# One table set for log and exp, copies of the first heads in two parts, and a second output bank, in an attention and FFN kernel

## The chip, the core and the metric

The kernel runs on one core of a Trainium2 chip. The metric is the device time of one launch in microseconds (us). The engines go by short names: PE is TensorE (PEld its weight loads), ACT is ScalarE, DVE is VectorE, POOL is GpSimd, SP is SyncE, which issues DMAs.

## The reference

Gated attention over 8 batches of 8 heads, 576 positions and 64 columns, and a SwiGLU block over its 4608 rows. In short:

```
scores = (q @ k.T) / sqrt(64)
cum    = cumsum(log(clip(f, 1e-4, 1)), axis=-1)
scores = where(causal, -1e9, scores + cum[:, None] - cum[None, :])
attn   = exp(scores - max); attn /= sum(attn) + 1e-9
x      = (attn @ v), heads side by side        # 4608 x 512
out    = (silu(x @ w_gate) * (x @ w_val)) @ w_out    # inner width 1536
```

Inputs and output are float32; the matmuls run in bfloat16.

## The kernel before

The program does not run loops on the chip. A planner in Python (`Plan`) takes some 1,600 operations with a list of what each waits for, an estimated cost on each engine that may run it, a key (its priority) and for some an earliest time (`ready`), and lays them out on the engines. What stands on an engine runs in that order; waits between engines are semaphores. The dictionary `ORDER` at the end overrides the keys of several hundred operations by number, so it fixes most of the order. Where the planner sees PE idle early on, it fills in warm-up matmuls (`dummy`, tile `idle`, L1272).

PSUM has eight banks, in the planner's pools: four `f` (`ps_119` to `ps_122`), two `s` for scores (`ps_123`, `ps_124`), one `o` for attention outputs (`ps_125`), one `t` for turned (transposed) tiles (`ps_126`).

The stages that matter here:

- Gates (`gates`): f is loaded, clipped on DVE, its log taken on ACT (L363), and summed by a scan on DVE (L367). DVE then makes rows (`hi`, `less`, `mid`, `low`, L372 to L383) that carry the sums as parts in bfloat16, so that matmuls can add them to the scores; `choose` (L392 on ACT, L394 on DVE) makes each head's rows for the second half. All of it is done in two parts, positions 0 to 255 and 256 to 575.
- Batch 0 takes a short way (`four`, `attention2`): POOL issues four loads (`ld_quad`, two head pairs each, tile `su`), k and q for g=0 and then for g=1; PE turns each in 64x64 pieces (`turn_two`, L563); ACT or DVE copies a turned bank of 576 columns straight into `QK` (`straighten_two`, L328 or L330). Scores of two heads at a time (`score2`, L722 to L734) need those copies and the gate rows. Block 0 of a head needs only positions 0 to 255 and the first part of the gates, and is done for all heads first (tiles `PTa`).
- After each score comes the exp on ACT (`expo`, L738), a causal mask on POOL (`mask`, L747), the product with V on PE (`weigh`, L761), then DVE takes the reciprocal (L768) and scales (L773), which frees the `o` bank. The result goes into `xT`, by PE (`flip`, L778) and a copy (`put`), or by DMA later on.
- Batches from 1 on: q and k are turned by PE (`quad`, batch 1) or by DMA; `attention` takes one head at a time, with four blocks of scores (L704).
- The FFN takes rows of `xT` in tiles of 512, 512 and 128: gate product (L919, `wg`), tanh on ACT (L930), value product (L919, `wv`), products on DVE, then the out product (L985 and others). Silu is made from tanh at first and by ACT's Silu later on. FFN work of earlier batches is laid between the attention of later ones, and fills PE.
- ACT works with one table set of functions at a time. Before, a warm-up activation with Ln (L523) and one with Exp (L531) make the compiler put the table loads there; tanh is in the second set.

The loads that the first 50 us need stand on POOL's queue between POOL's masks: q and k of batch 0, V of batch 0, `wv`, `wg` and `wo` in parts, q and k of batch 1, V of batch 1 (partly as casting loads, `ld_vb`, into tile `VB`).

Of the kernel before, what the change touches and what calls it, by code (L numbers as in the profile page):

```python
# [10 lines left out]
BF16 = mybir.dt.bfloat16  # L11
# [12 lines left out]
class Op:  # L24
    def __init__(self, eng, fn, after, behind, take, use, key, ready, dma):
        self.eng, self.fn, self.take, self.use = eng, fn, take, take + use
        self.key, self.ready, self.dma = key, ready, dma
        self.after = [a for a in after if a is not None]
        self.behind = list(behind)
        self.next, self.then, self.wait = [], [], 0  # L30
        self.start = self.done = None
        self.late = False


class Plan:
# [41 lines left out]
    def run(self, idle=None):  # L77
# [15 lines left out]
        left, t, seq = len(self.ops), 0.0, 0  # L93
# [15 lines left out]
        while left:  # L109
# [4 lines left out]
            while events and events[0][0] <= t + 1e-9:  # L114
                _, _, kind, o = heapq.heappop(events)
                if kind in ("queue", "dma"):
                    for r, share in shares():
                        r[0][0] -= (t - moved) * share
                        while r and r[0][0] < 1e-6:
# [3 lines left out]
                            n.done = t + 1.0  # L123
# [32 lines left out]
            for e in engines:  # L156
                while busy[e] <= t + 1e-9:
# [26 lines left out]
                    if o.dma is not None:  # L184
# [3 lines left out]
                        push(max(end + (0.53 if o.tag == "f" else 0.9), T_SW if e == "POOL" else 0.0), "queue", o)  # L188
# [33 lines left out]
def kernel(ctx, tc, q, k, v, f, w_gate, w_val, w_out, out):  # L222
# [82 lines left out]
    def op(eng, fn, *args, tag=None, packet=20.0, raw=0.0, **kw):  # L305
# [3 lines left out]
        o.tag, o.packet, o.raw = tag, packet, raw  # L309
        return o  # L310
# [109 lines left out]
    def gates(parts, key):  # L420
# [5 lines left out]
        for i, c in enumerate(parts):  # L426
            w = c.stop - c.start
            a = op(("DVE", 0.03 + w / 960), clip, lf[:D], c, after=lds, key=key - 1 + 0.1 * i, tag="clip")
            a = op(("ACT", 0.13 + w / 1100), ln, lf[D:], c, lf[:D], after=[a], key=key + 0.1 * i, tag="ln")
            lns.append(op(("ACT", 0.13 + w / 1100), ln, lf[:D], c, after=[a], key=key + 0.1 * i + 0.01, tag="ln"))  # L430
# [92 lines left out]
    o_ln = op(("ACT", 1.5), lambda e: nc.scalar.activation(warm, warm, AF.Ln), key=-30,  # L523
# [7 lines left out]
    o_warm = op(("ACT", 1.4), lambda e: nc.scalar.activation(warm, warm, AF.Exp), after=lns, key=WARM_KEY)  # L531
    o_rest = op(("DVE", 0.3), blank, "rest", key=QKZ_KEY + 0.1)
    o_vb = [op({"DVE": 0.4, "ACT": 0.6} if i == 1 else ("DVE", 0.4 if i else 0.12), blank, i, after=[o_ct] if i == 1 else [], key=(-29.5, VB1_KEY)[i] if i < FIRST else 40 + 2000 * i, ready=0 if i == 0 else 4.5 if i < FIRST else 15) for i in range(NVB)]
# [23 lines left out]

    def turn_two(e, jj, x, bt):
# [88 lines left out]
    def four(g, key):  # L647
# [3 lines left out]
        for j in range(2):  # L651
            jj = 2 * g + j
            q_ready[0, jj] = []
            for x in range(2):
                kk = key + STEP[j] + x
                bt = Buf("t", ("f", TURN_F))
                o2 = op(("PE", 0.22), turn_two, jj, x, bt, after=[o1[x], o_id], take=[bt], key=kk, tag=("turn", 0, jj, x))
                turns.append(o2)
                q_ready[0, jj].append(op({"ACT": act(S), "DVE": dve(S) - 0.02}, straighten_two, jj, x, bt, after=[o2, o_qkz],
                                         use=[bt, hq2[0][g]], key=kk, tag=("str", 0, jj, x)))  # L660

    def quad(b, g, key, ready=0.0):
        done = [[], []]
        for x in range(2):
            kk = key + x
            o1 = op(("POOL", SW), ld_quad, b, g, x, key=kk, dma=1.45, packet=107, ready=ready, tag=("quad", b, g, x))
            for n, (t0, nt) in enumerate(PH):
                bt = Buf("t", ("f", TURN_F))
                o2 = op(("PE", 1.48 * mm(*[P] * nt)), turn, b, g, x, n, bt, after=[o1, o_id], take=[bt], key=S1_KEY + kk, tag=("turn", b, g, x))
# [164 lines left out]
    def attention2(b, key, parts):  # L834

        bx = {}
        for n, (bks, qb, nq) in enumerate(parts):
            ahead = len(parts) > 1 and n == 0
            got = {}
            for jj in range(4):  # L840
# [4 lines left out]
                for m, i in enumerate(bks):  # L845
                    bs = [Buf("s", ("f", F_UNTIL)) for _ in range(2)]
                    segs = [x[2] for x in BANKS[i]]
                    cost = mm(*segs) * (3 if jj in (ONEHOT1 if i else ONEHOT) else 2) + 0.105
                    gate_rows = [o_past] + dec0[0][jj] + (dec0[1][jj] if i else [])
                    a = op(("PE", cost), score2, b, jj, i, bs, after=q_ready[b, jj] + gate_rows, take=bs,  # L850
# [30 lines left out]
    def attention(p, key):  # L881
# [3 lines left out]
        for j in range(2):  # L885
            h = 2 * p + j
            bo, ws, x1 = Buf("o"), [], None
# [169 lines left out]
    def unit(t, fc, t0, n, hs, lo, kk, after):  # L1057
# [16 lines left out]
        else:  # L1074
            b = op(("ACT", act(n)), tanh, n, bg, bt, after=[g], take=[bt], use=[bg], key=-5, tag=("tanh", t, fc))
# [227 lines left out]
def pool2(n):  # L1303
# [28 lines left out]
STEP = (0, 2)  # L1332
# [7 lines left out]
WARM_KEY = -19.5  # L1340
# [5 lines left out]
TURN_F = 48.0  # L1346
# [94 lines left out]
```

## Time and profile before

| what | value |
|---|---|
| three runs | 376.00, 376.13, 375.93 us; median 376.0 |
| profiled execution | 376.5 us, of it a span of 374.5 us |
| PE busy | 368.0 us (98%) |
| DVE, ACT, POOL busy | 256.9, 212.5, 169.5 us |
| weight loads (PEld) | 249.2 us |
| granted TensorE clock | 1.0 |

The span runs from the first instruction to the end of the last; the rest of the profiled execution lies around it. A row of the timeline gives start, length, engine, line, operation, output tile and input tile, and in brackets the idle time of the engine before it with what ended it. Where rows of one kind follow each other they are merged (x4). Consecutive activations overlap, so the cost of one in a row of them is the distance from start to start.

### The profile page before, as it was taken

The numbers are of one execution on the slowest core, as the hardware profiler recorded it, in microseconds if no ns is written. First come the engines' busy times: TensorE is split into PE (matmuls) and PEld (weight loads), VectorE is DVE, ScalarE is ACT, GpSimd is POOL, SyncE is SP. The second block draws the span as 40 slices with busy tenths as digits, with TensorE's granted clock in tenths as the row PEclk, the third lists the DMA queues.
The fourth block names the chain that finished last, engine by engine and source line by source line (L and its number), as shares of the span: only waits on it lengthen the run. The fifth ranks groups of instructions, "written<-read, shape, count | busy, mean of one in ns | idle before, by whom it ended". The sixth has DMA issues, their size and how long they took to land.

```text
span 374.5 us, 9689 instructions
## 1 busy us (share of the span) xinstructions
PE 368.0 (98%) x3715; PEld 249.2 (67%) x3715; DVE 256.9 (69%) x605; ACT 212.5 (57%) x436; POOL 169.5 (45%) x396
## 2 busy tenths in 40 slices
PE   7899999999999999999999999999999999999996
PEld 5667666455789646875578955587666964584586
DVE  7878987499937699548973769845888246617633
ACT  6999953256755647756566556676874233333321
POOL 8897554135565416684249533566440400040021
PEclk9999999999999999999999999999999999999999
DMA  8999998896959997999979999898530120011012
GB/s 144 190 200 194 206 217 143 169 215 121 174 106 234 212 161 111 170 221 181 200 152 200 126 234 196 155 150 212 105 38 19 58 84 2 1 58 56 0 57 86
DMA packets 125179, 52.04 MB, mean 139 GB/s; under 512 B 111838, under 2 KB 119582, under 8 KB 124366
## 3 DMA queue, kind: packets, MB, share of 16 engines
q1 hardware_dynamic: 108638, 36.15, 50.8%
q0 software_dynamic: 16288, 15.14, 27.1%
q8 instruction: 29, 0.48, 0.6%
q14 instruction: 16, 0.13, 0.1%
q10 hardware_dynamic: 208, 0.14, 0.1%
HBM read 38.56 MB, written 17.07 MB: 149 GB/s over the span
## 4 chain that ended last, share of the span: by engine, by line
PE 93%; ACT 3%; DVE 2%; issue 1%; POOL 0%; DVEq 0%; ACTq 0%
PE ps L919 43%; PE ps L985 17%; PE ps L704 10%; PE ps L761 8%; PE ps L926 6%; PE ps L998 3%; PE ps L992 3%; PE ps L722 1%; PE ps L579 1%; PE ps L778 1%; ACT PT L738 1%; ACT QK L328 1%; PE ps L730 0%; ACT xT L363 0%; ACT PTa L738 0%
## 5 line engine op out<-in xcount | busy, mean ns | idle before, releaser
L738 ACT ACTIVATE PT<-ps 128x384 bf16<-128x384 f32 (+2 forms) x192 | 90.8, 510 | 15.6 <-PE ps L704 10.7
L919 PE MATMUL ps<-xT,wv 128*128 128x512 bf16 (+1 forms) x400 | 99.3, 370 | 0.0
L919 PE MATMUL ps<-xT,wg 128*128 128x512 bf16 (+1 forms) x400 | 99.1, 370 | 0.0
L943 DVE SCALAR_TENSOR_TENSOR hh<-th,ps 128x512 bf16<-128x512 f32 (+1 forms) x100 | 65.9, 662 | 19.4 <-PE ps L919 15.9
L930 ACT ACTIVATE th<-ps 128x512 f32<-128x512 f32 (+1 forms) x82 | 47.2, 577 | 51.5 <-PE ps L919 44.8
L747 POOL TENSOR_SCALAR_AFFINE_SELECT PT<-PT 128x128 bf16<-128x128 bf16 (+1 forms) x192 | 54.6, 291 | 41.6 <-ACT PT L738 35.9
L940 DVE SCALAR_TENSOR_TENSOR th<-th,ps 128x512 f32<-128x512 f32 (+1 forms) x82 | 53.7, 655 | 14.7 <-ACT th L930 14.4
L704 PE MATMUL ps<-QK 68*128 68x256 bf16 x392 | 62.8, 261 | 0.1
L919 PEld LDWEIGHTS <-wg 128*128 128x128 bf16 x400 | 37.7, 97 | 34.2
L919 PEld LDWEIGHTS <-wv 128*128 128x128 bf16 x400 | 37.4, 97 | 34.5
L747 POOL TENSOR_SCALAR_AFFINE_SELECT PTa<-PTa 128x256 bf16<-128x256 bf16 x64 | 26.9, 423 | 63.9 <-ACT PTa L738 62.9
L976 DVE TENSOR_TENSOR su<-hh 128x512 bf16<-128x512 bf16 (+1 forms) x126 | 46.6, 404 | 1.0
L985 PEld LDWEIGHTS <-su 128*128 128x128 bf16 x420 | 40.4, 98 | 5.3
L761 PE MATMUL ps<-VB,PT 128*128 128x65 bf16 x768 | 41.4, 193 | 0.1
L704 PEld LDWEIGHTS <-QK 68*128 68x128 bf16 x392 | 31.8, 97 | 13.9 <-issue 0.3
L1018 POOL TENSOR_TENSOR ot<-ot 128x256 f32<-128x256 f32 x14 | 10.1, 724 | 63.8 <-ACT ot L1011 63.8
L761 PEld LDWEIGHTS <-PT 128*128 128x128 bf16 x768 | 34.1, 97 | 7.0 <-POOL PT L747 1.0
L738 ACT ACTIVATE PTa<-ps 128x384 bf16<-128x384 f32 x64 | 30.9, 488 | 12.6 <-PE ps L704 11.7
L933 ACT ACTIVATE th<-ps 128x512 f32<-128x512 f32 x30 | 17.9, 596 | 33.1 <-PE ps L919 27.7
L773 DVE TENSOR_TENSOR xn<-ps,rc 128x320 bf16<-128x320 f32 (+2 forms) x72 | 32.4, 453 | 2.1
L985 PE MATMUL ps<-wt,su 128*128 128x256 bf16 x252 | 32.9, 272 | 0.0
L1011 ACT ACTIVATE ot<-ps 128x512 f32<-128x512 f32 x28 | 16.7, 597 | 27.9 <-PE ps L985 26.5
(101 smaller groups left out, 407.0 us busy)
## 6 DMA issues: line engine op xcount, KB each, us to landing
out_dram<-ot SPq DMA_DIRECT2D x35, 256.0 KB
natv<-in_v_dram SPq DMA_DIRECT2D x25, 256.0 KB
qk_d<-in_q_dram POOLq DMA_DIRECT2D x24, 144.0 KB, 4.3
qk_d<-in_k_dram POOLq DMA_DIRECT2D x24, 144.0 KB, 4.8
wv<-in_moe_w_val_dram POOLq DMA_DIRECT2D x3, 512.0 KB, 10.7
wg<-in_moe_w_gate_dram POOLq DMA_DIRECT2D x3, 512.0 KB, 12.1
wo<-in_moe_w_out_dram POOLq DMA_DIRECT2D x4, 384.0 KB, 13.7
VB<-in_v_dram POOLq DMA_DIRECT2D x7, 128.0 KB, 9.1
```

Of the source, the lines that this page charges most:

```text
L704: nc.tensor.matmul(s[:, c : c + w], QK[:KR, hqk[p].i, 1, j * S + kt * P : j * S + (kt + 1) * P], QK[:KR, hqk[p].i, 0, j * S + q0 : j * S + ...
L738: nc.scalar.activation(place(h, i)[:, OFFS[i] : OFFS[i] + c], ps(bs)[:, :c], AF.Exp, scale=0.125)
L747: nc.gpsimd.affine_select(out=d, in_=d, pattern=pat, compare_op=ALU.is_ge, fill=0.0, base=0, channel_multiplier=-1,)
L761: nc.tensor.matmul(o[:, lo : lo + D + 1], pt[:, c : c + P], VB[hvb[b].i][:, kt, hb, : D + 1], start=first and n == 0, stop=last and n == l ...
L773: nc.vector.tensor_mul(XN[bx.i][:, qb : qb + nq, j], o, r)
L919: nc.tensor.matmul(ps(bf)[:, a:b], w[:, ko, fc * P : (fc + 1) * P], xT[:, ko, at : at + b - a], start=ko == 0 and a == 0, stop=ko == KD - ...
L926: nc.tensor.matmul(ps(bf)[:, c * P : (c + 1) * P], w[:, ko, (4 * fq + c) * P : (4 * fq + c + 1) * P], xT[:, ko, lo : lo + P], start=c + ko ...
L930: nc.scalar.activation(TH[bt.i][:, :n], ps(bf)[:, :n], AF.Tanh, scale=0.5)
L940: nc.vector.scalar_tensor_tensor(out=t, in0=t, scalar=1.0, in1=ps(bf)[:, :n], op0=ALU.add, op1=ALU.mult)
L943: nc.vector.scalar_tensor_tensor(out=HH[bh.i][:, r, lo : lo + n], in0=TH[bt.i][:, :n], scalar=by, in1=ps(bf)[:, :n], op0=ALU.mult, op1=ALU ...
L976: E[e].tensor_tensor(out=o, in0=x, in1=y, op=f)
L985: nc.tensor.matmul(ps(bf)[:, c * HALF : (c + 1) * HALF], left(g)[:, q * P : (q + 1) * P], right[:, g], start=opens and g == 0, stop=g == K ...
```

## The change

Seven things change.

1. The first table load is named: the set `natural_log_exp_and_others`, which has Ln and Exp, is loaded at the start in place of the Ln warm-up. The second named load, `exp_and_others`, is planned from 24 us on, after the logs, and is waited for by the first FFN tile's tanh instead of by batch 0's first exps. Both warm-up activations go.
2. Batch 0's straightening copies are made in two parts, 29 of 64 column groups (29 x 9 = 261 columns) and the other 35 (315). Block 0 waits for the first parts only.
3. The turns of batch 0 take any `f` bank until 48 us, or `t`, where they took `t` first.
4. From 112 us (planned) a head's output may take the `t` bank, if `o` is held.
5. The planner's costs change: some for the logs, clips and loads, 0.095 us for a change between kinds of matmul on PE, casting loads (POOL's queue) that land between 9 and 20 us counted 0.7 us later.
6. `ORDER` is replaced as a whole, so most operations up to the last tile stand in another order.
7. A way to turn two head pairs in one go (`turn_four`, `straighten_four`) is added; `JOINED = ()` leaves it unused.

As built, ACT has 11 copies of batch 0 (six of 261 columns, five of 315) where it had six of 576, DVE five (two and three) where it had two; ACT has two `choose` rows where it had one and one 320-column `put` less. PE has 43 warm-up matmuls where it had 46 and the same matmuls otherwise; the last 720 stand in the same order of kinds. ACT's second table load stands behind all 32 exps of batch 0 and ahead of the first tanh. On POOL, the five loads of batch 0's V stand ahead of the first `wv`, the second of the second pair of q and k is q, and the last k load of batch 1 stands further back.

```diff
@@ Plan.run
-                            n.done = t + 1.0
+                            n.done = t + 1.0 + (0.7 if n.ran == "POOL" and 9.0 < t < 20.0 else 0.0)
...
+                        dur += SWITCH * (o.shape != shape)
+                        shape = o.shape
...
-    o_ln = op(("ACT", 1.5), lambda e: nc.scalar.activation(warm, warm, AF.Ln), key=-30,
+    o_ln = op(("ACT", 1.35), lambda e: nc.scalar.preload_act_table_set("natural_log_exp_and_others"), key=-30,
...
-    o_warm = op(("ACT", 1.4), lambda e: nc.scalar.activation(warm, warm, AF.Exp), after=lns, key=WARM_KEY)
+    o_warm = op(("ACT", 1.35), lambda e: nc.scalar.preload_act_table_set("exp_and_others"), after=lns, key=WARM_KEY, ready=WARM_AT)
...
+    EARLY = -(-HALF // QT)
...
-    def straighten_two(e, jj, x, bt):
+    def straighten_two(e, jj, x, c0, c1, bt):
         g, j = divmod(jj, 2)
-        dst = QK[:, hq2[0][g].i, x, j * S : (j + 1) * S].rearrange("p (c t) -> p c t", t=QT)
-        copy(e, dst, ps(bt).bitcast(BF16)[:, :S].rearrange("p (t c) -> p c t", t=QT))
+        dst = QK[:, hq2[0][g].i, x, j * S : (j + 1) * S].rearrange("p (c t) -> p c t", t=QT)[:, c0:c1]
+        copy(e, dst, ps(bt).bitcast(BF16)[:, :S].rearrange("p (t c) -> p c t", t=QT)[:, c0:c1])
@@ four
-                bt = Buf("t", ("f", TURN_F))
+                bt = Buf(*T_BANKS)
...
+                for m, (c0, c1) in enumerate(((0, EARLY), (EARLY, QP))):
...
+                        q_ready.setdefault((0, 2 * g + j), ([], []))[m].append(c)
@@ soft
-        a = x = op(("ACT", act(cols)), expo, h, i, bs, after=[a] + ([x1] if i > 1 else []) + ([o_warm] if h < H and not i else []),
+        a = x = op(("ACT", act(cols)), expo, h, i, bs, after=[a] + ([x1] if i > 1 else []),
@@ attention2
-                    a = op(("PE", cost), score2, b, jj, i, bs, after=q_ready[b, jj] + gate_rows, take=bs,
+                    a = op(("PE", cost), score2, b, jj, i, bs, after=q_ready[b, jj][0] + (q_ready[b, jj][1] if i else []) + gate_rows, take=bs,
@@ attention
-            bo, ws, x1 = Buf("o"), [], None
+            bo, ws, x1 = Buf("o", ("t", T_FREE, 1e9)), [], None
@@ unit
-            b = op(("ACT", act(n)), tanh, n, bg, bt, after=[g], take=[bt], use=[bg], key=-5, tag=("tanh", t, fc))
+            b = op(("ACT", act(n)), tanh, n, bg, bt, after=[g] + ([o_warm] if t == 0 else []), take=[bt], use=[bg], key=-5, tag=("tanh", t, fc))
@@ constants
-STEP = (0, 2)
+TURN_F = 48.0
+JOINED = ()
+COPY_ON = ("DVE", "ACT")
+T_FREE = 112.0
+T_BANKS = (("f", TURN_F), "t")
+SWITCH = 0.095
-WARM_KEY = -19.5
+WARM_KEY = -5.5
+WARM_AT = 24.0
 ORDER = {
...
```

More of the change, by code (lines that the diff above doesn't have):

```diff
@@ L31, in __init__ @@
         self.start = self.done = None
-        self.late = False
+        self.late, self.shape = False, None
 class Plan:
@@ L92, in run @@
         rings, moved = {"SP": [], "ACT": [], "POOL": []}, 0.0
-        left, t, seq = len(self.ops), 0.0, 0
+        left, t, seq, shape = len(self.ops), 0.0, 0, None
         events = []
@@ L187, in run @@
                         taken[k] += 1
-                        push(max(end + (0.53 if o.tag == "f" else 0.9), T_SW if e == "POOL" else 0.0), "queue", o)
+                        push(max(end + (0.73 if o.tag == "f" else 0.9), T_SW if e == "POOL" else 0.0), "queue", o)
                         push(busy[e], "wake", None)
@@ L309, in op @@
         o.tag, o.packet, o.raw = tag, packet, raw
+        o.shape = tag[0] if "PE" in eng and tag[0] in ("s2", "turn") else None
         return o
@@ L427, in gates @@
             w = c.stop - c.start
[L428 to L430 removed]
+            a = op(("DVE", 0.12 + w / 960), clip, lf[:D], c, after=lds, key=key - 1 + 0.1 * i, tag="clip")
+            a = op(("ACT", 0.18 + w / 980), ln, lf[D:], c, lf[:D], after=[a], key=key + 0.1 * i, tag="ln")
+            lns.append(op(("ACT", 0.18 + w / 980), ln, lf[:D], c, after=[a], key=key + 0.1 * i + 0.01, tag="ln"))
         for i, c in enumerate(parts):
@@ L650, in four @@
             o_id.behind.extend(o1)
[L651 to L655, printed above, removed]
-                bt = Buf("t", ("f", TURN_F))
-                o2 = op(("PE", 0.22), turn_two, jj, x, bt, after=[o1[x], o_id], take=[bt], key=kk, tag=("turn", 0, jj, x))
-                turns.append(o2)
-                q_ready[0, jj].append(op({"ACT": act(S), "DVE": dve(S) - 0.02}, straighten_two, jj, x, bt, after=[o2, o_qkz],
-                                         use=[bt, hq2[0][g]], key=kk, tag=("str", 0, jj, x)))
+        for x in range(2):
+            for n in range(2):
+                kk = key + x + 2 * n
+                bt = Buf(*T_BANKS)
+                if g in JOINED:
+                    o2 = op(("PE", 1.48 * mm(*[P] * PH[n][1]) - 0.09), turn_four, g, x, n, bt, after=[o1[x], o_id], take=[bt], key=kk, tag=("turn", 0, g, x, n))
+                else:
+                    o2 = op(("PE", 0.25), turn_two, 2 * g + n, x, bt, after=[o1[x], o_id], take=[bt], key=kk, tag=("turn", 0, g, x, n))
+                turns.append(o2)
+                for m, (c0, c1) in enumerate(((0, EARLY), (EARLY, QP))):
+                    w = (c1 - c0) * (2 * PH[n][1] if g in JOINED else QT)
+                    fn, args = (straighten_four, (g, x, n, c0, c1, bt)) if g in JOINED else (straighten_two, (2 * g + n, x, c0, c1, bt))
+                    on = {"ACT": act(w), "DVE": dve(w) - 0.02}
+                    c = op({COPY_ON[x]: on[COPY_ON[x]]} if g in JOINED else on, fn, *args, after=[o2, o_qkz],
+                           use=[bt, hq2[0][g]], key=kk + 50 * m, tag=("str", 0, g, x, n, m))
+                    for j in range(2) if g in JOINED else [n]:
+                        q_ready.setdefault((0, 2 * g + j), ([], []))[m].append(c)
     def quad(b, g, key, ready=0.0):
@@ L668, in quad @@
                 bt = Buf("t", ("f", TURN_F))
-                o2 = op(("PE", 1.48 * mm(*[P] * nt)), turn, b, g, x, n, bt, after=[o1, o_id], take=[bt], key=S1_KEY + kk, tag=("turn", b, g, x))
+                o2 = op(("PE", 1.48 * mm(*[P] * nt) - 0.09), turn, b, g, x, n, bt, after=[o1, o_id], take=[bt], key=S1_KEY + kk, tag=("turn", b, g, x))
                 turns.append(o2)
@@ L1345 @@
 V_CAST = {0: 5, 1: 3}
-TURN_F = 48.0
 DEC1_KEY = 1000
```

15 lines of the change are left out of this document (13 added, 2 removed), and 117 rows, old and new, of the table ORDER.

## Prediction

> **What bounds the kernel now.** I read the page first, then busy time by stage, then the timeline of the first 30 us, then the places where TensorE (PE) stands still later on. The page:
>
> ```profile
> span 374.5 us, 9689 instructions
> ...
> PE 368.0 (98%) x3715; PEld 249.2 (67%) x3715; DVE 256.9 (69%) x605; ACT 212.5 (57%) x436; POOL 169.5 (45%) x396
> ...
> PE 93%; ACT 3%; DVE 2%; issue 1%; POOL 0%; DVEq 0%; ACTq 0%
> ```
>
> PE has 368.0 of the 374.5 us and carries 93% of the chain that ended last. No edit takes a real matmul away: of the instructions on PE only three warm-up ones (L1272) go, 46 to 43. So only time in which PE stands still, warms up or waits can be won. The stages (window, PE, then weight loads, DVE, ACT, POOL):
>
> ```profile
> 0.00:16.00 16.00, 13.23 (x243) 9.90 (x245) 12.70 (x49) 12.38 (x26) 13.86 (x25) 1.00 1.24 162
> 16.00:36.00 20.00, 19.63 (x338) 13.96 (x333) 16.64 (x66) 19.68 (x45) 16.71 (x43) 1.00 1.42 196
> 36.00:112.00 76.00, 76.00 (x684) 48.00 (x683) 58.93 (x125) 43.74 (x95) 37.53 (x92) 1.00 0.92 169
> 112.00:288.00 176.00, 175.58 (x1793) 119.91 (x1791) 126.96 (x278) 110.81 (x231) 89.42 (x226) 1.00 0.94 164
> ```
>
> From 36 us PE is full: 76.00 of 76.00, then 175.58 of 176.00. Until then ScalarE (ACT) is the fullest engine: 19.68 of 20.00 us between 16 and 36. So the path runs over ACT to about 36 us and over PE from there; what ACT gains ahead of 36 us moves everything behind it. The last 720 matmuls stand in the same order in both kernels, so the end gives nothing. ACT's timeline and what feeds it (start, length, engine, line, operation; in brackets the idle time before it):
>
> ```profile
> 7.48 2.38 ACT L328 ACTIVATE QK<-ps 128x576 bf16<-128x576 bf16 x4
> ...
> 7.69 0.10 PEld L563 LDWEIGHTS <-su 64*64 64x64 bf16 x1 [0.78 <-DMA su<-in_q_dram]
> 8.05 0.40 DVE L360 TENSOR_SCALAR ot<-ot 128x216 f32<-128x216 f32 x1
> 8.16 0.66 PE L563 MATMUL ps<-ident,su 64*64 64x64 bf16 x36 [0.96 <-ACT QK L328]
> ...
> 8.38 0.86 DVE L367 TENSOR_TENSOR_SCAN xT<-xT 128x320 f32<-128x320 f32 x1
> ...
> 9.28 0.81 DVE L372 TENSOR_SCALAR xT<-xT 128x320 bf16<-128x320 f32 x1
> ...
> 9.40 0.34 PE L722 MATMUL ps<-QK 64*128 64x256 bf16 x4
> ...
> 9.74 0.38 ACT L363 ACTIVATE ot<-ot 128x216 f32<-128x216 f32 x1
> ...
> 10.14 1.28 ACT L531 ACT_TABLE_LOAD   x1
> ...
> 11.44 0.20 ACT L531 ACTIVATE warm<-warm 1x1 f32<-1x1 f32 x1
> 11.54 0.75 DVE L330 COPY QK<-ps 128x576 bf16<-128x576 bf16 x1
> 11.55 0.46 ACT L738 ACTIVATE PTa<-ps 128x384 bf16<-128x384 f32 x1
> 11.92 0.62 ACT L328 ACTIVATE QK<-ps 128x576 bf16<-128x576 bf16 x1
> ...
> 12.20 0.64 DVE L383 SCALAR_TENSOR_TENSOR xT<-xT,ct 128x320 bf16<-128x320 f32 x1
> 12.45 0.46 ACT L738 ACTIVATE PTa<-ps 128x384 bf16<-128x384 f32 x1
> ...
> 13.35 0.64 ACT L392 ACTIVATE xT<-xT,ct 128x320 bf16<-128x320 f32 x1
> ...
> 13.89 0.83 ACT L738 ACTIVATE PTa<-ps 128x384 bf16<-128x384 f32 x2
> ...
> 15.01 0.21 PE L733 MATMUL ps<-one,xT 64*128 64x128 bf16 x1 [0.68 <-issue]
> ...
> 15.31 1.82 ACT L738 ACTIVATE PTa<-ps 128x384 bf16<-128x384 f32 x4 [0.58 <-PE ps L734]
> ...
> 17.02 9.46 ACT L738 ACTIVATE PT<-ps 128x512 bf16<-128x512 f32 x22
> ...
> 26.54 0.44 ACT L328 ACTIVATE xT<-ps 128x320 bf16<-128x320 bf16 x1
> ...
> 29.00 0.37 ACT L930 ACTIVATE th<-ps 128x256 f32<-128x256 f32 x1
> ```
>
> The first scores begin at 9.40, but ACT loads the second table from 10.14 and the first exp runs at 11.55. Between 14.72 and 15.31 ACT idles 0.58 us: PE stood 0.68 us inside the second pair of scores (15.01), as I read it for a bank that the exps from 13.89 on were emptying. From 15.31 ACT runs on with hardly a gap; the first tanh is at 29.00.
>
> **Part by part.** All of it is costed on the profiled execution: 376.5 us, a span of 374.5 and 2.0 around it. The three runs have a median of 376.0, so I take the difference from there.
>
> *Table sets.* Both kernels load three tables. The second load moves from ahead of the first exp to behind the 32nd and last exp of batch 0, ahead of the first tanh. That takes 1.28 us away before 11.55 and puts 1.28 us back near 27 us, where ACT is as full. The warm-up activation goes: 11.44 to 11.55, 0.11 us won on ACT. Queued behind the moved load are the first tanh and the straightening copies of batch 1; PE waits for the tanh only once the banks of the gate products run out.
> The load's length is the row's: 1.28 us, and the idle time ahead of it is 10.14 less 9.74 and 0.38, that is 0.02 us. The Trainium skill, ScalarE: Activation LUTs, section What ACT_TABLE_LOAD costs, counts 1.28 us for the load and 1.38 us more for a drain at every change of set; the trace agrees with the first and shows nothing of the second. By the page's sum the moved load would save 2.66 us ahead of the first exp and cost 2.66 behind the last.
>
> *Copies in two parts.* Six ACT copies of 576 columns become six of 261 and five of 315; two of 576 on DVE become two of 261 and three of 315. ACT goes from start to start in 0.53 us with 576 columns (11.92 to 12.45) and 0.37 with 384 (11.55 to 11.92): 0.83 ns a column and 0.05 us fixed. So 6 x 0.27 + 5 x 0.315 = 3.2 us against 6 x 0.53 = 3.2: nothing, as DVE takes a part over. DVE went from start to start in 0.66 us with 576 columns (11.54 to 12.20). A part of 261 is between 0.30 (in proportion) and 0.66; I take 0.35, and 0.40 for 315, near the low end as ACT's fixed share is small too. DVE then does 1.9 us of copies for 1.3, ahead of 16 us, where it has 12.70 of 16.00. Block 0 needs only the first parts. Before, the turn of the first q waited until 8.16 for the bank that ACT had to empty, though the data were there at 7.69; now every turn has a bank of its own (four f banks, or t). The first scores then wait for DVE, which does the clip at 8.05, then two copies of 261 at 0.35 each: 9.1 instead of 9.40.
>
> *Exps.* Without the load, ACT ends its log at about 9.8 and starts the first exp there, 1.7 us earlier. The second q and k cannot land earlier (their loads stay third and fourth on POOL's queue), so the second scores gain less. In the new order ACT has ahead of the fifth exp four exps, four copies of 261, one of 315 and two gate rows (L392): 4 x 0.37 + 4 x 0.27 + 0.315 + 2 x 0.54 = 4.0 us from 9.8, so 13.8 against 15.31. The 0.58 us of idle time go, since these scores now take the s banks, which the first two exps have emptied. Four exps later (15.31 to 17.02 before, 1.7 us) the first exp of later blocks comes at 15.4 to 15.5 instead of 17.02, a lead of 1.6 us.
>
> *DVE's chain.* Those exps need the second half of the gate rows. On DVE the two copies of 261 now stand between the clip (8.05) and the scan (8.38), and two copies of 315 and two gate rows inside the chain, which ended at 12.84 (12.20 and 0.64); one copy of 576 leaves it. 2 x 0.35 + 2 x 0.40 - 0.66 for the copies, and for the gate rows 2 x 0.54 by ACT's row (the same columns): 12.84 + 1.9 = 14.8. It keeps up with 15.4 by 0.6 us, of which the scores take part.
>
> *ACT's sum to 36 us.* Load 0; warm-up -0.11; idle time -0.58; copies 0; one gate row more on ACT +0.54 (13.35 to 13.89); one 320-column put moved to DVE -0.44 (26.54). Sum -0.59 us. That the lead of 1.6 us comes down to 0.6 is the load paid later and the gate row. Bounds: -1.6 if PE finds enough other work during the load, +0.8 if the lead is lost (below).
>
> *Loads.* V of batch 0 now lies wholly ahead of the weights; wg stays behind wv and one q load of batch 1, with a k load moved behind it; the last k load of batch 1 moves on POOL's queue behind two V loads and sixteen masks, where it had two masks ahead of it.
>
> ```profile
> L919 PE MATMUL ps<-xT,wg x44: 269/272/380, 28.3 to 44.0; 128*128 128x256 bf16 x32, 128*128 128x512 bf16 x12
> L910 POOL DMA_DIRECT2D wg<-in_moe_w_gate_dram x3: 747/773/780, 12.4 to 31.6; - x3
> ...
> DMA to landing us min/median/max: 12.0/12.1/12.6
> ```
>
> wg is issued at 12.4, lands 12.0 us later at 24.4 and is first used at 28.3: 3.9 us of cover, and one 288 KB load fewer stands ahead of it. Cost nothing; without that cover PE waits as long as it is late. The last k load is needed only behind the first eight gate products of four matmuls, so after wg; by the same 12 us it lands near 32 if issued near 20. Cost nothing, +1 us at worst. The casting loads of V of batch 1 are issued later, behind most weights; the blocks that need them stand last in their head's products.
>
> *Second output bank.* From 112 us heads use the turns' bank for their outputs too. Before, each head opens the only o bank behind DVE's scaling of the head before. Where that was late:
>
> ```profile
> 129.48 0.49 DVE L773 TENSOR_TENSOR xn<-ps,rc 128x320 bf16<-128x320 f32 x1
> ...
> 130.03 0.12 PEld L761 LDWEIGHTS <-PTa 128*128 128x128 bf16 x2 [0.41 <-issue]
> ...
> 146.00 0.12 PEld L761 LDWEIGHTS <-PTa 128*128 128x128 bf16 x2 [0.19 <-issue]
> ...
> 150.45 0.12 PEld L761 LDWEIGHTS <-PTa 128*128 128x128 bf16 x2 [0.17 <-issue]
> ...
> 188.50 0.12 PEld L761 LDWEIGHTS <-PTa 128*128 128x128 bf16 x2 [0.20 <-issue]
> ...
> 274.07 0.21 PEld L761 LDWEIGHTS <-PT 128*128 128x128 bf16 x5 [0.27 <-POOL PT L747]
> ```
>
> The scaling ends at 129.97, the matmul goes on at once. The four gaps make 0.41 + 0.19 + 0.17 + 0.20 = 0.97 us, of which a weight load's 0.1 each would stand anyway: 0.6 us to win. The wait for a mask at 274.07 (0.27) is not of this kind and stays, and the new order sets some products a little closer behind their scores. I take -0.4, between -0.6 and +0.6 (two more mask waits of 0.3).
>
> Sum: -0.59 - 0.4 = -1.0 us: 375.5 in the profiled execution's terms, **375.0 us** against the median.
>
> **The rivals.**
> *The lead stays* (0.20): PE, not ACT, paces the stretch from 26 us, as the 19.63 of 20.00 us of PE also allow; the load hides behind products that are due anyway. Then -1.6 - 0.5 = -2.1: 373.9. Against it: ACT's 19.68.
> *Nothing is left* (0.17): ACT's idle time comes back at another bank (+0.58), and new mask waits eat the 0.4. Then 375.0 + 1.0 = 376.0.
> *Drain at the load* (0.05): an idle ACT ahead of the moved load while its pipeline empties, in the fullest stretch. Bounded by the row's 0.02 and, as a mechanism here, by the length of the load itself, 1.3: 375.0 + 1.3 = 376.3. By the Trainium skill's page above it would be 1.38 us.
> *Slower: DVE's chain is late* (0.20). The place is the copies ahead of the scan. If the low rows (L383, second half) end after about 16.5 instead of 14.8, the exps of later blocks begin no earlier than 17.0; the lead is gone while the load is still paid: +1.28 + 0.3 for the exps that shift - 0.44 - 0.11 = +1.0, and with -0.1 left of the bank 376.9. For it: the row at 9.28 took 0.81 us for 320 columns, more than the copy of 576 at 11.54, so DVE can be held up there; and DVE takes three more pieces.
>
> **How the numbers follow.** My forecast has 0.38; its own range, 374.6 to 375.5, is the ACT sum between -0.9 and -0.3 with the bank at its value. The range 373.7 to 376.9 reaches from the lead that stays to the late chain. A difference under 0.2% (0.75 us) is about what a measurement of this kernel can tell from no change. Faster by more, below 375.25: the lead and 0.30 of the forecast's 0.38, together 0.50. Within: the other 0.08 of the forecast, nothing left and the drain, 0.30. Slower, above 376.75: the late chain, 0.20.
>
> **What would show it.** First exp near 9.8 (11.0 would be a miss); first 512-column exp at 15.4 to 15.6; no idle ACT of 0.5 us between 13 and 17; table load at about 26 to 27 us with under 0.1 us of idle time ahead; first tanh within 1 us of before's 29.0; DVE's second low row ended by 15.0; no weight-load gaps behind DVE's scaling beyond 112 us. Wrong it is if the first 512-column exp comes after 16.5, if PE stands for a tanh behind the load for more than 1 us, or if mask waits past 112 us make more than 1.5 us.

## Result and the profile after

The changed kernel takes 374.36 us (median of 5 runs, 374.0 to 375.43) against 376.0 (375.9 to 376.43): a ratio of 0.9959, interval 0.9943 to 0.9975. Run again on another chip it gave 0.9969 (0.9958 to 0.9980). So it gains between 1.2 and 1.6 us; 1.0 was forecast. The profiled execution took 374.4 us, with a span 1.9 us shorter than before's. In some executions below, the clock granted to PE has a mean of 0.991 to 0.995 instead of 0.999 or 1.0 (full clock here), and before then has a median of 376.98 us (14 executions) against 376.23 (71), so differences at full clock stand beside the ratios.

The page, and busy time by stage (window, PE, weight loads, DVE, ACT, POOL):

```profile
span 372.6 us, 9646 instructions
...
PE 364.1 (98%) x3678; PEld 248.3 (67%) x3712; DVE 256.8 (69%) x608; ACT 212.7 (57%) x439; POOL 170.6 (46%) x396
...
16.00:36.00 20.00, 19.75 (x337) 15.15 (x334) 17.60 (x68) 19.84 (x44) 16.19 (x41) 1.00 1.33 200
...
112.00:288.00 176.00, 174.78 (x1771) 120.23 (x1789) 128.47 (x282) 109.97 (x230) 89.18 (x224) 1.00 0.92 161
```

ACT is still full between 16 and 36 us (19.84 of 20.00, 19.68 before). (Some matmul records are missing from this trace: 3678 beside 3712 weight loads. So its PE sums say nothing.) What changed is what ACT's full time holds. ACT's timeline:

```profile
8.73 0.76 ACT L331 ACTIVATE QK<-ps 128x315 bf16<-128x315 bf16 x2 [0.33 <-DVE QK L333]
...
9.65 0.87 ACT L762 ACTIVATE PTa<-ps 128x384 bf16<-128x384 f32 x2
...
11.78 0.39 ACT L331 ACTIVATE QK<-ps 128x261 bf16<-128x261 bf16 x1 [0.34 <-DVE QK L333]
...
14.10 0.53 ACT L762 ACTIVATE PTa<-ps 128x384 bf16<-128x384 f32 x1
14.84 1.25 ACT L762 ACTIVATE PTa<-ps 128x384 bf16<-128x384 f32 x3 [0.21 <-PE ps L758]
15.98 9.84 ACT L762 ACTIVATE PT<-ps 128x512 bf16<-128x512 f32 x24
25.84 1.28 ACT L534 ACT_TABLE_LOAD   x1
27.13 0.39 ACT L954 ACTIVATE th<-ps 128x256 f32<-128x256 f32 x1
27.41 1.53 ACT L331 ACTIVATE QK<-ps 64x640 bf16<-64x640 bf16 x2
```

The first exp comes at 9.65 instead of 11.55, the first 512-column exp at 15.98 instead of 17.02, and the first tanh at 27.13 instead of 29.00, though the whole table load of 1.28 us now stands ahead of it. ACT stands for 0.33, 0.34 and 0.21 us on the way. The load is entered without a pause: 24 exps end at 25.82, the load starts at 25.84.

PE and DVE ahead of 16 us, from the timeline of all engines:

```profile
8.75 0.34 PE L746 MATMUL ps<-QK 64*128 64x256 bf16 x4
...
10.66 1.08 DVE L333 COPY QK<-ps 128x315 bf16<-128x315 bf16 x2
...
13.94 0.55 DVE L386 SCALAR_TENSOR_TENSOR xT<-xT,ct 128x320 bf16<-128x320 f32 x1
...
14.24 0.23 PE L746 MATMUL ps<-QK 64*128 64x128 bf16 x2 [0.29 <-issue]
```

Scores start at 8.75 (9.40 before). DVE's second low row ends at 14.49. PE still stands inside the second pair of scores, for 0.29 us where it was 0.68.

Two profiles of one kernel differ too. In the second one of the changed kernel (span 373.5 us) the first tanh comes at 27.92. There the fourth q and k load landed at 11.19 us instead of 10.70. So 0.8 us of the difference between the two profiles first shown can be chance; where single profiles and times disagree, the times below decide.

### The profile page after: what moved, and what is told of

Its sections match the earlier page's. It is cut to its first block, busy times and chain, and to the rows that moved or that the text cites. A ratio compares the mean times of both kernels' runs of the same rounds, so it can differ in the third digit from the quotient of the medians.

```text
span 372.6 us, 9646 instructions
## 1 busy us (share of the span) xinstructions
PE 364.1 (98%) x3678; PEld 248.3 (67%) x3712; DVE 256.8 (69%) x608; ACT 212.7 (57%) x439; POOL 170.6 (46%) x396
## 4 chain that ended last, share of the span: by engine, by line
PE 71%; issue 0%; ACT 0%; POOL 0%; DVE 0%
PE ps L943 33%; PE ps L1009 17%; PE ps L728 8%; PE ps L950 6%; PE ps L785 5%; PE ps L1022 3%; POOL PTa L771 0%; ACT PTa L762 0%; ACT PT L762 0%; DVE ot L333 0%; PE ps L802 0%
## 5 line engine op out<-in xcount | busy, mean ns | idle before, releaser
L762 ACT ACTIVATE PT<-ps 128x512 bf16<-128x512 f32 (+2 forms) x192 | 90.4, 518 | 21.2 <-PE ps L728 16.4
L943 PE MATMUL ps<-xT,wv 128*128 128x512 bf16 (+1 forms) x386 | 97.8, 370 | 0.8
L943 PE MATMUL ps<-xT,wg 128*128 128x512 bf16 (+1 forms) x384 | 96.9, 370 | 0.8
L728 PE MATMUL ps<-QK 68*128 68x256 bf16 x392 | 64.0, 261 | 0.4 <-ACT PTa L762 0.2
L785 PE MATMUL ps<-VB,PT 128*128 128x65 bf16 x768 | 43.2, 193 | 0.1
L785 PEld LDWEIGHTS <-PT 128*128 128x128 bf16 x768 | 36.3, 97 | 9.3 <-POOL PT L771 1.0
L728 PEld LDWEIGHTS <-QK 68*128 68x128 bf16 x392 | 31.9, 97 | 12.8 <-issue 0.6
```

The source lines that it names most:

```text
L728: nc.tensor.matmul(s[:, c : c + w], QK[:KR, hqk[p].i, 1, j * S + kt * P : j * S + (kt + 1) * P], QK[:KR, hqk[p].i, 0, j * S + q0 : j * S + ...
L762: nc.scalar.activation(place(h, i)[:, OFFS[i] : OFFS[i] + c], ps(bs)[:, :c], AF.Exp, scale=0.125)
L785: nc.tensor.matmul(o[:, lo : lo + D + 1], pt[:, c : c + P], VB[hvb[b].i][:, kt, hb, : D + 1], start=first and n == 0, stop=last and n == l ...
L943: nc.tensor.matmul(ps(bf)[:, a:b], w[:, ko, fc * P : (fc + 1) * P], xT[:, ko, at : at + b - a], start=ko == 0 and a == 0, stop=ko == KD - ...
```

## Experiments

The theory of the prediction: ACT paces the kernel to 36 us, so the load costs the same wherever it stands, and the gain is idle time and a bank. The rival that the profile favours: the late load stands where ACT would have waited anyway. The twelve runs, with before and the first measurement, stand in one table; the ratio is to before on the same chip. The third column compares medians at full clock with before's on the same chip (4 to 12 executions of each variant). The start of the 17th tanh tells how the head went; the time from the 33rd to the 81st tanh holds most of the part in which the second output bank works. Single profiles scatter there: before and e7, whose work is in the same order, have 74.1 and 73.4 for the 17th tanh.

| kernel | ratio, interval | at full clock, us | 17th tanh, us | 33rd to 81st, us |
|---|---|---|---|---|
| before | 1 | 0 | 74.1 | 158.2 |
| after, first time | 0.9959 (0.9943 to 0.9975) | -1.6 | 72.4 | 157.7 |
| r_after: after again | 0.9969 (0.9958 to 0.9980) | -1.1 | 73.2 | 157.6 |
| e1: after, load early | 0.9982 (0.9971 to 0.9993) | -0.7 | 74.4 | 157.6 |
| e2: after, three loads | 1.0047 (1.0031 to 1.0062) | +1.1 | 75.4 | 158.3 |
| e3: after, one output bank | 0.9974 (0.9961 to 0.9988) | -1.1 | 72.2 | 158.1 |
| e4: after, whole copies | 0.9969 (0.9958 to 0.9980) | -0.8 | 73.3 | 157.8 |
| e8: after, load at tile 1 | 0.9962 (0.9951 to 0.9973) | -1.6 | 74.1, behind the load | 157.6 |
| e10: after, e1 + e3 + e4 | 0.9989 (0.9975 to 1.0003) | -0.7 | 73.2 | 158.4 |
| e11: after, a bank's copies on one engine | 1.0023 (1.0011 to 1.0036) | +0.8 | 74.5 | another order |
| e5: before, load late | 1.0028 (1.0017 to 1.0039) | +1.4 | 75.1 | 157.9 |
| e7: before, turns on the f banks | 0.9999 (0.9989 to 1.0009) | -0.2 | 73.4 | 158.2 |
| e9: before, e5 + e7 | 1.0013 (1.0005 to 1.0022) | +0.8 | 75.1 | 157.9 |
| e6: before, second output bank | 0.9974 (0.9962 to 0.9986) | -0.6 | 74.2 | 157.2 |

The changed kernel run once more was the yardstick of its variants:

> The changed kernel once more, as the mark for the others on the same chip: 0.994 to 0.998 of before in every theory.

### e1: the load back ahead of the first exp

```diff
@@ after: the planned operation emits nothing, the first exp emits the load
-    o_warm = op(("ACT", 1.35), lambda e: nc.scalar.preload_act_table_set("exp_and_others"), after=lns, ...)
+    o_warm = op(("ACT", 1.35), lambda e: None, after=lns, ...)
@@ expo
+        if not loaded:
+            loaded.append(nc.scalar.preload_act_table_set("exp_and_others"))
```

> The changed kernel (374.4 us) with one instruction moved: the load of the second table set stands ahead of the first exp again, and no longer ahead of the first tanh; every other instruction stands where it did on its engine. Theory A, the sum on record (ACT paces everything to about 36 us, so 1.28 us cost the same in both places): the first 512-column exp at about 17.3 instead of 16.0, the first tanh as before the edit, 374.1 to 374.7. Theory B (behind about 25 us PE is the pace and hides the late load): the first tanh stays near 27.1, but the exps and the products behind them run 1.0 to 1.3 later, 375.3 to 375.7.

Measured 0.9982: some 0.5 us slower than the changed kernel's second run, 0.9 than its first. The interval overlaps that of the second run; at full clock the medians are 375.49 and 375.15 us. ACT behind the last exps:

```profile
27.71 0.38 ACT L958 ACTIVATE th<-ps 128x256 f32<-128x256 f32 x1
29.38 1.55 ACT L331 ACTIVATE QK<-ps 64x640 bf16<-64x640 bf16 x2 [1.29 <-DVE rc L796]
```

and PE and DVE just before, in the timeline of all engines:

```profile
28.87 0.47 PE L596 MATMUL ps<-ident,xT 128*64 128x128 bf16 x10
...
29.19 0.17 DVE L796 RECIPROCAL rc<-ps 128x3 f32<-128x3 f32 x1
```

Where the late load stood, ACT now waits 1.29 us. The bracket names DVE's reciprocal, the last event before; what the copy reads is the turn of batch 1 that PE starts at 28.87 and ends at 29.34. So the load's room became a wait for PE. What stands ahead of 17 us in this profile can't be compared directly: the granted clock was 0.50 from 12.8 to 16.2 us, behind a wait of PE of 1.26 us, and 18 turns of PE that start at 12.90 took 0.69 us, not 0.47 as in the changed kernel. Half of e1's ten executions have a mean clock of 0.995, as this one; what brings the stretch on is not shown. The hole stands in e8 and e10 too, whose profiles are at full clock there. That the load costs less in the late place is what the times favour; how much less, they leave open between 0.3 and 0.9 us.

### e8: the load taken out of that place in another way

The first 16 tanh (tile 0's) are done as exps here, which need no new set, and the load stands ahead of the 17th; that tile's silu is thereby another function.

```diff
@@ tanh
+        made.append(n)
+        if len(made) == 17:
+            nc.scalar.preload_act_table_set("exp_and_others")
-        nc.scalar.activation(TH[bt.i][:, :n], ps(bf)[:, :n], AF.Tanh, scale=0.5)
+        nc.scalar.activation(TH[bt.i][:, :n], ps(bf)[:, :n], AF.Exp if len(made) < 17 else AF.Tanh, scale=0.5)
```

> The changed kernel with the second table load moved out of the head: the first FFN tile's 16 tanh are replaced by exp (so that tile's values are others), which the first set has, and the load stands ahead of the second tile's first tanh, near 72 us, where ACT has idle time; all else in its order. Theory A (ACT is the pace around 26 us): 1.0 to 1.3 us less than the changed kernel. Theory B (PE's products cover one load there, as the first tanh that came only 0.6 us later in the kernel with the early load suggests): within 0.3 us of the changed kernel, with ACT idle in the load's place.

Measured 0.9962, between the changed kernel's two ratios. Its profile and the second one of the changed kernel have the fourth load landing alike (11.10 and 11.19 us). First e8, then the changed kernel again:

```profile
26.51 0.38 ACT L959 ACTIVATE th<-ps 128x256 f32<-128x256 f32 x1
28.08 1.54 ACT L331 ACTIVATE QK<-ps 64x640 bf16<-64x640 bf16 x2 [1.19 <-DVE rc L792]
```

```profile
26.63 1.28 ACT L534 ACT_TABLE_LOAD   x1
27.92 0.38 ACT L954 ACTIVATE th<-ps 128x256 f32<-128x256 f32 x1
28.20 1.53 ACT L331 ACTIVATE QK<-ps 64x640 bf16<-64x640 bf16 x2
```

Without the load the tanh comes 1.41 us earlier, and then ACT waits 1.19 us; the copies of batch 1 start at 28.08 against 28.20. Of these 0.12 us none need be the load's: e8's tanh starts 0.12 us ahead of the other kernel's load already (26.51, 26.63), and PE's turn for the copies 0.09 us ahead (27.57, 27.66). The load takes 1.28 us of ACT and next to nothing of the work behind it.

### e2: three loads there

```diff
+    def load2(e):
+        nc.scalar.preload_act_table_set("exp_and_others")
+        nc.scalar.preload_act_table_set("natural_log_exp_and_others")
+        nc.scalar.preload_act_table_set("exp_and_others")
-    o_warm = op(("ACT", 1.35), lambda e: nc.scalar.preload_act_table_set("exp_and_others"), after=lns, ...)
+    o_warm = op(("ACT", 1.35), load2, after=lns, ...)
```

> The changed kernel with three table loads in a row where it has one ahead of the first tanh, all else in its order: 2.56 us more on ACT at 25.8 us. Theory A: the whole 2.56 us reaches the end, 376.7 to 377.1. Theory B: PE has products to go on with and only what exceeds its cover shows, between 0 and 1.3 us, 374.4 to 375.7, with the first tanh at 29.7.

Measured 1.0047, that is 0.0078 (2.9 us) above the changed kernel's second run, for 2.56 us of added loads. At full clock (four executions) the median is 377.35 us, 2.2 above the second run's 375.15.

```profile
26.36 1.28 ACT L535 ACT_TABLE_LOAD   x1
27.65 1.28 ACT L536 ACT_TABLE_LOAD   x1
28.94 1.28 ACT L537 ACT_TABLE_LOAD   x1
30.23 0.38 ACT L959 ACTIVATE th<-ps 128x256 f32<-128x256 f32 x1
```

The room holds one load. What comes on top of it shows in full or nearly so, and ACT does pace the kernel there as soon as the room is used up.

### e5 and e9: the late load in the old order

e5 is the kernel before with the two named sets only, its order kept; e9 adds e7's banks.

```diff
@@ e5, before
-    o_ln = op(("ACT", 1.5), lambda e: nc.scalar.activation(warm, warm, AF.Ln), key=-30,
+    o_ln = op(("ACT", 1.5), lambda e: nc.scalar.preload_act_table_set("natural_log_exp_and_others"), key=-30,
...
-    o_warm = op(("ACT", 1.4), lambda e: nc.scalar.activation(warm, warm, AF.Exp), after=lns, key=WARM_KEY)
+    o_warm = op(("ACT", 1.4), lambda e: None, after=lns, key=WARM_KEY)
@@ the first tanh
+        if not loaded:
+            loaded.append(nc.scalar.preload_act_table_set("exp_and_others"))
@@ e7, and in e9 on top of e5: four
-                bt = Buf("t", ("f", TURN_F))
+                bt = Buf(("f", TURN_F), "t")
```

> The kernel before with the table sets of the changed one and nothing else: the set with log and exp is loaded at the start, the second set is loaded ahead of the first tanh instead of ahead of the first exp, the two warm-up activations are gone; every other instruction stands in before's order. Theory A: 0.1 to 0.4 us less than before, 375.6 to 375.9. Theory B, if the table set alone brings the gain: 1.0 to 1.5 us less, 374.5 to 375.0. A third: before's order cannot use it, since its second scores wait for copies and banks that come no earlier: no difference, 376.0 or a little above, as the load then stands in the middle of its exps.

> The kernel before with one edit: batch 0's turns take f banks first and t last; every instruction stands in before's order, only bank numbers differ. My account: the turn of the first q starts when its data land (about 0.5 us earlier), but in before the exps wait for the table load anyway, so 0 to 0.3 us less than before. Rival: the banks alone bring a good part of the gain, 0.6 us or more.

> The kernel before with its order of work kept, to which two parts of the change are done together: the second table load behind batch 0's exps, and the turns of batch 0 on the f banks first. The late load alone was slower by 1.05 us, the banks alone were worth nothing. Theory B1 (the late load fails in the old order because copies and scores there wait for one bank, which keeps ACT from using the time it gained): both together are at 0.9985 to 1.0000, the first 512-column exp by 15.6 us. Theory B2 (it fails because the old order has no other work to lay beside the load or ahead of it, whatever the banks): 1.0020 to 1.0035 as without the banks, the first 512-column exp near 16.5 us and the first tanh near 30.0.

The late load alone makes the old kernel slower: 1.0028. The banks alone do nothing (0.9999), and with them the late load is still slower (1.0013). The ACT timelines of e5 and e9 agree to 0.06 us in what follows; e5's:

```profile
10.20 0.49 ACT L738 ACTIVATE PTa<-ps 128x384 bf16<-128x384 f32 x1 [0.47 <-PE ps L734]
...
14.80 1.82 ACT L738 ACTIVATE PTa<-ps 128x384 bf16<-128x384 f32 x4 [0.74 <-PE ps L734]
16.50 9.39 ACT L738 ACTIVATE PT<-ps 128x512 bf16<-128x512 f32 x22
...
27.91 0.72 ACT L328 ACTIVATE QK<-ps 64x512 bf16<-64x512 bf16 x1
28.66 1.28 ACT L933 ACT_TABLE_LOAD   x1
29.95 0.38 ACT L934 ACTIVATE th<-ps 128x256 f32<-128x256 f32 x1
```

The first exp is 1.35 us earlier than before, the first 512-column exp only 0.52: in the old order ACT spends the rest waiting for PE's scores (0.47 and 0.74 us). Then the load stands behind the copies of batch 1, not ahead of them, and it shows: the first tanh is 0.95 us later than before, and in e5 PE stands 0.69 us at 31.14 for an ACT copy behind it. Before's first log is 0.39 us later than e5's, so part of the lead is chance. Against e7, which has e9's order and banks and a first log within 0.06 us, e9's first exp is 0.86 us earlier (10.14, 11.00), but its first 512-column exp 0.25 us later (16.50, 16.25), as is its fourth load (10.63, 10.38). The expectation that the banks were to blame fell; it is the order.

### e10: what the new order is worth without the parts

The diff is those of e1, e3 and e4 together.

> The changed kernel with three of its parts taken back at once: the second table load stands ahead of the first exp again, the copies of batch 0 are whole, outputs keep to their one bank. What is left of the change is the new order of work, the turns' f banks and the costs. Theory of parts that add up: the changed kernel's -1.2 us, and 0.5 (load) + 0.1 (copies) + 0.2 (bank) taken back: -0.4 us against before, ratio 0.9988 to 0.9992. Theory of the order (the new order alone pays, the parts only ride on it): 0.9968 to 0.9980. Theory of the parts (the order alone is worth nothing or less, it was laid out for the late load): 1.0000 to 1.0025.

Measured 0.9989 (0.9975 to 1.0003), as the sum of the parts had it; the interval does not exclude nothing. At full clock, though (ten of its twelve executions), the median is 375.60 us against before's 376.25: the new order with the turns' banks brings 0.65 us there, over half of the 1.1 of the changed kernel's second run. That it brings all is out. Its ACT has the same hole as e1's:

```profile
26.50 0.38 ACT L961 ACTIVATE th<-ps 128x256 f32<-128x256 f32 x1
28.19 1.55 ACT L331 ACTIVATE QK<-ps 64x640 bf16<-64x640 bf16 x2 [1.30 <-DVE rc L799]
```

So the late load costs 0.5 us or more in the old order (1.0013 to 1.0028). In the new one it wins 0.3 to 0.9 by the times of e1; e10 is 0.5 us slower than e3 at full clock (375.60, 375.10), which has the late load and copies in parts, and one output bank as e10. These differences are small for the scatter, and one pair of profiles shows nothing of them: e10 and the changed kernel's second profile, whose fourth loads landed alike (11.14 and 11.19 us), start the copies of batch 1 at 28.19 and 28.20 and the 17th tanh at 73.2 both. So the load alone does not pay, the order alone pays in part, and what the late load adds in the new order is likely but not settled.

### e4 and e11: the copies

e4 copies a bank of batch 0 whole on the engine that had its first part. e11 keeps the parts but gives both to one engine, where ACT and DVE shared four banks.

```diff
@@ e4: straighten_two
+        if c0:
+            return
+        c1 = QP
@@ e11: four
+                    if (2 * g + n, x) in ONE:
+                        on = {ONE[2 * g + n, x]: on[ONE[2 * g + n, x]]}
...
+ONE = {(0, 0): "DVE", (2, 0): "DVE", (2, 1): "ACT", (3, 1): "ACT"}
```

> The changed kernel with batch 0's copies whole again: the first part's copy takes all 576 columns (on the engine and at the place of the first part), the second part's instruction is gone; all else in its order. My account: the first scores wait for two whole copies on DVE, 0.3 to 0.6 us later, the first exp near 10.2, ACT's total unchanged: 374.7 to 375.0. Rival: the copies in two parts do nothing, since the second scores wait for later loads anyway: 374.2 to 374.6.

> The changed kernel in which both parts of a turned bank of batch 0 are copied by the same engine, where four banks were shared by ACT and DVE (two go wholly to DVE, two wholly to ACT); the planner lays the order anew behind them. If ACT's waits of 0.33 and 0.34 us for DVE's copy of the same bank cost time that reaches the end: 0.3 to 0.7 us below the changed kernel, a ratio to before of 0.994 to 0.996. If they only take slack away that ACT has ahead of 26 us: as the changed kernel, 0.9962 to 0.9975. If the order laid anew costs more than the waits: above 0.998.

e4 has the ratio of the changed kernel's second run, 0.9969 both (at full clock 375.45 and 375.15 us, six executions each): the two parts are worth nothing that could be measured, as forecast. e11 tells nothing of its question. The planner laid everything behind the copies anew:

```profile
12.96 0.99 ACT L331 ACTIVATE QK<-ps 128x261 bf16<-128x261 bf16 x3 [0.66 <-PE ps L568]
...
26.12 1.28 ACT L534 ACT_TABLE_LOAD   x1
27.42 0.49 ACT L764 ACTIVATE PT<-ps 128x384 bf16<-128x384 f32 x1
27.81 0.38 ACT L956 ACTIVATE th<-ps 128x256 f32<-128x256 f32 x1
```

ACT's waits for DVE went, and 0.66 us for a turn of PE came instead. The first tanh is as early as the changed kernel's (27.81), but the 17th is not (74.5), so its time is lost behind the load, in the order laid anew, and what the waits cost stays open.

### e3 and e6: the second output bank

```diff
@@ e3, after
-T_FREE = 112.0
+T_FREE = 1e9
@@ e6, before: attention
-            bo, ws, x1 = Buf("o"), [], None
+            bo, ws, x1 = Buf("o", ("t", 112.0, 1e9)), [], None
```

> The changed kernel without the second output bank (heads wait for the one o bank to the end); nothing is moved ahead of 112 us, some instructions are laid out anew behind. My account: the waits at heads' first products come back, 0.4 to 0.6 us more than the changed kernel, all of it between 112 and 288 us. Rival: the bank brings nothing that shows, within 0.15 us of the changed kernel, and the whole gain is from the head.

> The kernel before, in which a head's output may take the turns' bank from 112 us on (planned), and nothing else; the order of work behind that point is laid anew by the planner. Theory A (the prediction's term of -0.4 us): 0.3 to 0.5 us below before, a ratio of 0.9987 to 0.9992, and the stretch from 112 to 288 us shorter by as much, with the weight loads behind DVE's scaling (0.41, 0.19, 0.17 and 0.20 us before) gone. Rival: the waits are replaced by others (masks, score banks), 0, ratio 0.9997 to 1.0003, with the stretch as long as before.

In the old order the bank alone brings 0.9974, 0.8 us between the medians (375.61 and 376.43) and 0.6 at full clock (376.25), more than the 0.4 that was forecast for it. Its head is before's to within 0.04 us from the fifth exp to the 33rd tanh, so the profile shows the bank, with the order that the planner lays anew behind it: 1.0 us from the 33rd to the 81st tanh. In the new order taking the bank away costs 0.0005, which is inside the scatter; in the profiles it is 0.4 to 0.5 us. Gaps ahead of weight loads of the products with V from 120 to 152 us, in the changed kernel, in e3 and in e6:

```profile
128.55 0.24 PEld L785 LDWEIGHTS <-PT 128*128 128x128 bf16 x4 [0.25 <-POOL PT L771]
...
144.58 0.14 PEld L785 LDWEIGHTS <-PTa 128*128 128x128 bf16 x3 [0.20 <-POOL PTa L771]
...
148.84 0.21 PEld L785 LDWEIGHTS <-PT 128*128 128x128 bf16 x5 [0.18 <-POOL PT L771]
```

```profile
128.49 0.13 PEld L785 LDWEIGHTS <-PTa 128*128 128x128 bf16 x2 [0.41 <-issue]
...
145.79 0.12 PEld L785 LDWEIGHTS <-PTa 128*128 128x128 bf16 x2 [0.28 <-issue]
...
149.00 0.20 PEld L785 LDWEIGHTS <-PT 128*128 128x128 bf16 x5 [0.18 <-POOL PT L771]
```

```profile
129.92 0.24 PEld L761 LDWEIGHTS <-PT 128*128 128x128 bf16 x4 [0.25 <-POOL PT L747]
...
150.09 0.20 PEld L761 LDWEIGHTS <-PT 128*128 128x128 bf16 x5 [0.18 <-POOL PT L747]
```

Before's gaps of 0.41, 0.19 and 0.17 us behind DVE's scaling become one of 0.25 and one of 0.18 for masks in e6. In the new order the bank turns 0.41 and 0.28 into 0.25 and 0.20, both for masks. From 112 to 288 us all such gaps above 0.15 us make 1.8 us before and 1.7 in e6, where waits for masks of 0.25 to 0.27 us stand at 262, 264, 270 and 276 us; in the new order they make 1.5 and 1.3 in the changed kernel's two profiles, 1.9 in e3 and 2.2 in e10. So e6's 1.0 us does not stand in these gaps, and where it comes from is not shown; nor is the difference between 1.0 and 0.4.

## Why the prediction was right, and where it was wrong

The direction and the range held; the gain was 0.2 to 0.6 us larger than forecast. The forecast's own range, 374.6 to 375.5, has the second measurement (0.9969 of 376.0 is 374.8) and just misses the first (374.36); from the bounds that it names, -0.9 and -0.3 with -0.4 for the bank, it would be 374.7 to 375.3. By its steps:

- *The load, 0.* This step failed. It said that the load is put back where "ACT is as full". ACT is full there because the load fills it: e1, e8 and e10 have 1.2 to 1.3 us of idle time in that place, and e8 shows next to nothing of the 1.28 reaching the next copies. The busy share of a stage was read as if it belonged to the place; it belonged to the old order, in which e5 shows the load exposed. The rival "the lead stays" had this mechanism: work of PE that is due anyway covers the load. It had a chance of 0.20 and 373.9 us; the first measurement lies between it and the forecast.
- *No drain.* Right. The idle time ahead of the moved load is 0.02 us, and e2's loads follow each other every 1.29 us. The Trainium skill, ScalarE: Activation LUTs, section What ACT_TABLE_LOAD costs, adds 1.38 us of drain to a change of set; no trace here shows it.
- *Idle ACT, -0.58.* Wrong in size and, by this profile, in sign: of the 0.58 us 0.21 are left, but waits of 0.33 and 0.34 came, 0.88 in all. The prediction saw the new s banks, and PE's stop in the scores did shrink, from 0.68 to 0.29 us. It did not see that ACT's copy of one part waits for DVE's copy of the other part of the same bank.
- *First exp 9.8, fifth 13.8, first of later blocks 15.4 to 15.6.* 9.65, 14.10 and 15.98 (16.24 in the second profile). The first was right; from there the waits above make the difference, and the lead at the 512-column exps is 0.8 to 1.0 us against the profile before, and not 1.6 (less still against e7, which has before's order and 16.25). That the lead is smaller and the load cheaper than forecast offset each other in part, which is why the sum came out near: that is luck. (The step from a lead of 1.6 us down to 0.6 counts the gate row twice; it is in the 4.0 us ahead of the fifth exp already. Less the load, with the put added, 1.6 leaves 0.76, not the sum's 0.59.)
- *First tanh within 1 us of 29.0.* 27.13 and 27.92: missed, for the reason of the load. (e7, in before's order, has 28.26, so chance makes part of it.)
- *Copies, 0; scores at 9.1; DVE's low row by 14.8.* e4 bears out the first; 8.75 and 14.49 the others. DVE's chain kept up, so the slower rival had no place.
- *Choose row +0.54 and put -0.44.* Both are as built; nothing tested them alone.
- *Loads.* The view of waits has one for PE from 16 to 112 us, and that for an exp; no load was late:

```profile
PE ps L728 <- ACT PTa L762: 0.2, 1, 0.2
```

- *Second output bank, -0.4.* Right for the new order, by the profiles (0.4 to 0.5); the times do not resolve it. That it is worth more in the old order (0.6 to 0.8) was not foreseen: the gaps ahead of weight loads, from which it was costed, do not hold what e6 gained.

## What to carry to other kernels

A stage in which an engine is busy 98% of the time may still have room for an operation, if another order of work puts it where that engine would wait for a second one: look for what the engine would do next without the operation, and when its input is there. A moved operation and the order around it are one change; here the late load alone lost time, and the order alone brought some 0.65 us of 1.1 to 1.6. Before an output buffer's wait is costed from visible gaps alone, try the second buffer by itself: it was the smallest edit here, and alone in the old order it brought about half of the whole change's gain.

## What was not expected of the hardware

In two places ACT did not copy its part of a PSUM bank while DVE copied the other part: it waited 0.33 us (8.73) and 0.34 us (11.78, where DVE's copies from 10.66 end at 11.74), and with e11's one engine for a bank both waits are gone. The Trainium skill, PSUM — Partial Sum Buffer, section PSUM bank collisions raise a hardware error, says that the compiler's scheduler puts a dependency between instructions on different engines that touch one bank in the same 32-partition quadrant, reads too; these two waits agree with it.

Two starts vary from run to run. The first log starts at 3.94 to 4.00 us in most profiles and at 4.33 or 4.34 in three (before, e2, e4). The fourth q and k load lands between 10.38 and 11.42 us, and where the order depends on it everything behind moves with it: the changed kernel's two profiles are 0.9 us apart. That is more than half of what the change brings, so one pair of profiles could not have measured it.
